# Spread inverses as one transfer per row, and the banks of attention in another order

## The chip, the cores and the metric

The kernel runs on one core of a Trainium2 chip. Its time is the device time of one execution in microseconds (us); the number that counts is the median over executions. Engines are named as in the profile: PE (matmul), PEld (its weight loads), DVE, ACT and POOL (elementwise), SP (here only the issuer of transfers). PSUM, PE's output memory, has eight banks of 128 x 512 float32; every score tile or value tile takes one bank. Transfers between memory and on-chip storage run on 16 DMA engines.

## The reference, cut to what matters

Two attention paths of 16 heads of width 28 over the same 2048 tokens, mixed by a gate. Path A is linear attention, path B softmax attention.

```
def _A_ref(x, wqkv, w_phi, wo):
    ...
    phi_q = concat([softmax(pq), softmax(-pq)]);  phi_k = concat([softmax(pk), softmax(-pk)])
    kv  = einsum("bhsf,bhsd->bhfd", phi_k, v)
    num = einsum("bhqf,bhfd->bhqd", phi_q, kv)
    den = einsum("bhqf,bhf->bhq", phi_q, z)[..., None] + 1e-6
    return merge_heads(num / den) @ wo
def _B_ref(x, wqkv, wo):
    p = softmax(einsum("bhqd,bhkd->bhqk", q, k) * scale)
    return merge_heads(einsum("bhqk,bhkd->bhqd", p, v)) @ wo
g = sigmoid((x * gate_w).sum(-1, keepdims=True))
return g * a + (1 - g) * b
```

## The kernel before

The kernel has three stages. The first (to about 62 us) loads the tokens, splits them into high and low parts and projects queries and keys of path B, which go to memory (`qkd`). The second (62 to 356 us) computes path A token tile by token tile. In its gaps it runs `mx_unit`, which finds the row maxima of path B's scores: PE's `pmd` and `pmb` tiles (L260), ACT's `rl` (L264), DVE's reduction into `part` (L265). Towards its end it computes path B's values (`value_b`, tiles `pvb`, copied out by ACT into `vb`, L699). The third (from 356 us) is attention of path B: scores (`score`, L874), exponentials (L882), remaining row maxima (L288, L295), value products (`values`, L1019), normalisation and the output projection.

The order of work on PE, DVE, ACT and POOL is the order of the code, written out by hand; each engine works through its queue in that order. The order of the transfers on SP is set by a scheduler.

**Path A's normalisation.** Query tiles (128 tokens) are handled in eight pairs. For each pair `numer` computes numerators and denominators into two tiles `pn` (L529), 256 tokens and all heads: a tile has four groups of 32 rows, one head each, of which row 28 is the denominator. `normalize1` copies the tiles to `oU` on ACT (L381) and fetches the denominators by two small transfers into `den` (L384). `normalize2` inverts them on DVE (L389), writes them to a small buffer `rd` in memory, 4 rows of 1024 inverses (L393, two transfers), and spreads them back: `rs` has 128 rows, and each of the 4 rows of `rd` is read 32 times, 512 KB in all (L394). `normalize3` multiplies `oU` by `rs` on DVE (L400). `normalize4` splits the result into high (ACT, L408) and low (POOL, L409) halves, which `out_a` multiplies with the output weights (`poa`, L544). In names of the profile an `a` is added for path A: `dena`, `rda`, `rsa`. Path B uses the same functions for one tile at a time (n = 1, names with `b`); its transfer of 256 KB is a single one before and after. In between, the queues hold other work of path A: query projection (`pq`, L109, copied by ACT to `pcq`, L421), the features `featq` (DVE L423, L424, L443 to L445, POOL L429, L431, L446, ACT's exponential L434), their transposes (`pft`, L516, copied by ACT to `fT`, L519).

**The banks.** Each stage opens its own pool of PSUM tiles. A tag gets its bank when it is first named, and a new pool hands out the banks in turn; the first instruction that writes a bank waits for the last reader of what the old pool had there. In the old pool, the two banks of tag `s` hold the value tiles by turns, and the six of tag `mx` hold those of `mx_unit` and the first four score tiles (`st0`). In the new pool there is `pv` for the value product, and `g0` to `g6`, handed out by the list `free`. The first attention step with scores of its own (s = 1) uses `g0`, `g1`, two row-maximum tiles in `g2` and `g3`, scores in `g4` and `g5`, and a row-maximum tile in `g6`. `pv` is first written by `values(0)`, behind the scores of step 2.

Of the kernel before, what the change touches and what calls it, by code (L numbers as in the profile page):

```python
# [41 lines left out]
def gated_mix_kernel(ctx, tc, xT, wqkB, wvB, wvA, wkAT, wqAT, phi, woA, woB,  # L42
# [7 lines left out]
    nc = tc.nc  # L50
# [336 lines left out]
    def normalize2(pool, oU, den, nm, n):  # L387

        nc.vector.reciprocal(den, den)  # L389
        rd = dr.tile([4, n * 512], F32, tag=f"rd{n}", name=f"rd{nm}", bufs=2)  # L390
        rs = pool.tile([P, n, 512], F32, tag="rs", name=f"rs{nm}", bufs=n)
        for k in range(n):
            nc.sync.dma_start(rd[:, k * 512:(k + 1) * 512], den[:, k, :])  # L393
        nc.sync.dma_start(rs.rearrange("p n q -> p (n q)"),  # L394
                          rd.unsqueeze(1).to_broadcast([4, 32, n * 512]))
        return oU, rs

    def normalize3(oU, rs, n):
# [312 lines left out]
    for i in range(2 * NT + 11):  # L711
        t, q = i, i - NT
# [47 lines left out]
        if y >= 6 and y % 2 == 0 and tb - 3 < 8:  # L760
            num[tb - 3] = normalize2(ta, *num[tb - 3], f"a{tb - 3}", 2)
# [198 lines left out]
    def bank(i, nm):  # L960
        return ps2.tile([P, 512], F32, tag=f"g{i}", name=nm, bufs=1)
# [2 lines left out]
        free.append(free.pop(0))  # L964
        return bank(free[-1], nm)

    for i in (0, None, 1, 6, 5, 4, 3, 2):
        if i is None:
            ps2.tile([P, 512], F32, tag="pv", name="pv_first", bufs=1)
        else:  # L970
            bank(i, f"first{i}")
# [83 lines left out]
    def finish(gq, s):  # L1055
# [8 lines left out]
        def f2():  # L1064
            st["n"] = normalize2(late_p, *st["n"], f"b{gq}", 1)
# [189 lines left out]
```

## Time and profile before

| | us |
|---|---|
| median of 3 executions | 982.85 (982.53 to 985.76) |
| the profiled execution, its time | 983.95 |
| its span, first to last instruction | 982.2 |
| PE busy | 971.7 (99%) |
| ACT busy | 751.9 (77%) |
| DVE busy | 715.5 (73%) |
| POOL busy | 230.6 (23%) |

The durations below come from the profiled execution. A matmul's end is modelled, and matmuls overlap, so a busy PE isn't a PE at its peak; what counts is where it waits, and which wait ends last. The mean granted clock of PE over the span is 0.998 of the full one. In a view of stretches the two figures behind the busy times are the granted clock and the share of the 16 DMA engines that is busy.

### The profile page before, as it was taken

What the parts mean: (1) busy time and instruction counts of PE and PEld (TensorE: products, weight loads), DVE (VectorE), ACT (ScalarE), POOL (GpSimd) and SP (SyncE); (2) the same over time, 40 slices, a digit from 0 to 9 for tenths busy, and PEclk for the clock granted to TensorE, in tenths of its full rate; (3) what the DMA queues carried; (4) which work ended last, traced back from release to release, by engine and by line L of the source; (5) the groups of instructions that cost most, each with busy time, mean ns of one, the idle gap of its engine ahead of it and who ended that gap; (6) DMA issues with size and microseconds to landing.
All of it is one profiled execution on the core that took longest, in us unless ns stands there. A gap on an engine that the chain in (4) does not pass through costs nothing.

```text
span 982.2 us, 22550 instructions
## 1 busy us (share of the span) xinstructions
PE 971.7 (99%) x8510; PEld 602.5 (61%) x8510; DVE 715.5 (73%) x1337; ACT 751.9 (77%) x1442; POOL 230.6 (23%) x237
## 2 busy tenths in 40 slices
PE   9999999998999999999999999999999999999998
PEld 8877877786777655555555555555555555555555
DVE  5476767886755678888888888888888888885112
ACT  5455656586876679889889889889889888887662
POOL 1235535586634800031011011011011011010010
PEclk9999999999999999999999999999999999999999
DMA  8973010112233333121122121122231222100441
GB/s 307 321 244 114 32 54 32 58 36 78 71 115 109 93 119 118 39 58 46 65 86 73 37 61 45 59 79 68 67 83 42 66 61 67 38 21 31 141 150 57
DMA packets 56140, 84.49 MB, mean 86 GB/s; under 512 B 17216, under 2 KB 23984, under 8 KB 56032
## 3 DMA queue, kind: packets, MB, share of 16 engines
q1 hardware_dynamic: 56032, 83.06, 26.9%
q8 instruction: 67, 1.10, 0.4%
q14 instruction: 41, 0.34, 0.1%
HBM read 54.86 MB, written 27.78 MB: 84 GB/s over the span
## 4 chain that ended last, share of the span: by engine, by line
PE 95%; DVE 2%; DMA 1%; ACT 1%; issue 0%; SPq 0%; POOL 0%; DVEq 0%; POOLq 0%; ACTq 0%
PE g L874 29%; PE pv L1019 26%; PE pqk L109 6%; PE poa L544 4%; PE pk L127 4%; PE pva L127 4%; PE g L288 3%; PE pmd L260 3%; PE pob L109 3%; PE pq L109 2%; PE pvb L127 2%; PE pvb L109 2%; PE pqk L635 1%; DMA rsa<-rda 1%; PE pft L516 1%; PE pkv L468 1%
## 5 line engine op out<-in xcount | busy, mean ns | idle before, releaser
L882 ACT ACTIVATE p<-g 128x512 f32<-128x512 f32 x1020 | 525.8, 610 | 83.9 <-PE g L874 83.2
L295 DVE TENSOR_REDUCE part<-g 128x1 f32<-128x512 f32 x704 | 442.6, 684 | 84.9 <-PE g L288 83.0
L874 PEld LDWEIGHTS g<-qst,kst 32*128 32x128 f32 x3060 | 221.3, 182 | 216.4 <-DVE part L295 194.7
L874 PE MATMUL g<-qst,kst 32*128 32x512 f32 x3060 | 338.1, 419 | 1.1 <-ACT vb L699 0.9
L1019 PE MATMUL pv<-p,vb 128*32 128x512 f32 x2048 | 273.0, 604 | 0.0
L288 PE MATMUL g<-kc,qc 28*128 28x512 f32 x704 | 233.3, 494 | 0.0
L265 DVE CUSTOM_DVE_ANT_0 rl<-pmb,rl 128x512 f32<-128x512 f32 x160 | 103.4, 684 | 51.0 <-ACT rl L264 51.0
L400 POOL TENSOR_TENSOR oUb<-oUb,rsb 128x512 f32<-128x512 f32 x15 | 19.3, 1289 | 494.4 <-DMA rsb<-rdb 462.4
L264 ACT ACTIVATE rl<-pmd 128x512 f32<-128x512 f32 x160 | 87.5, 603 | 31.0 <-PE pmb L260 30.1
L288 PEld LDWEIGHTS g<-kc,qc 28*128 28x128 f32 x704 | 86.2, 181 | 0.2
L1019 PEld LDWEIGHTS pv<-p,vb 128*32 128x32 f32 x2048 | 40.5, 108 | 66.2 <-issue 64.9
L109 PE MATMUL pqk<-XH,wB 128*128 128x512 f32 x192 | 59.1, 396 | 0.0
L544 PE MATMUL poa<-woA_s,oTa 128*128 128x448 f32 x192 | 45.7, 386 | 0.0
L573 ACT CAST ev<-pqk 128x512 fp32r<-128x512 f32 x28 | 16.1, 588 | 38.6 <-PE pqk L109 29.6
L1030 DVE SCALAR_TENSOR_TENSOR acc<-pob,gate,acc 128x448 f32<-128x448 f32 x12 | 8.2, 684 | 48.4 <-PE pob L109 48.4
L260 PE MATMUL pmb<-kp,qp 28*128 28x512 f32 x160 | 42.1, 495 | 0.1
L574 DVE TENSOR_TENSOR ev<-pqk,ev 128x512 fp32r<-128x512 f32 x28 | 19.1, 690 | 30.7 <-ACT ev L573 30.7
L109 PEld LDWEIGHTS pqk<-XH,wB 128*128 128x128 f32 x192 | 35.4, 188 | 8.5 <-issue 1.2
L544 PEld LDWEIGHTS poa<-woA_s,oTa 128*128 128x128 f32 x192 | 35.9, 195 | 7.2 <-issue 3.7
L260 PE MATMUL pmd<-kp,qp 28*128 28x512 f32 x160 | 40.0, 494 | 0.0
L127 PE MATMUL pk<-wkA_s,XH 128*128 128x448 f32 x128 | 39.4, 381 | 0.0
L127 PE MATMUL pva<-wvA_s,XH 128*128 128x450 f32 x128 | 37.8, 371 | 0.0
(158 smaller groups left out, 1056.3 us busy)
## 6 DMA issues: line engine op xcount, KB each, us to landing
qkd<-ev SPq DMA_DIRECT2D x28, 512.0 KB
qst<-qkd SPq DMA_DIRECT2D x64, 112.0 KB
kst<-qkd SPq DMA_DIRECT2D x64, 112.0 KB
od<-oTb SPq DMA_DIRECT2D x48, 112.0 KB
rsa<-rda SPq DMA_DIRECT2D x8, 512.0 KB
oL<-od SPq DMA_DIRECT2D x8, 512.0 KB
rsb<-rdb SPq DMA_DIRECT2D x15, 256.0 KB
gad<-ga SPq DMA_DIRECT2D x16, 224.0 KB
```

The costliest lines, as they stand in the source:

```text
L109: nc.tensor.matmul(dst, l, r, start=i == 0, stop=i == len(todo) - 1)
L127: nc.tensor.matmul(dst[:, :n], l, r, start=i == 0, stop=i == len(todo) - 1, skip_group_check=True)
L260: nc.tensor.matmul(pm[j], qc[js, qt * P:(qt + 1) * P], kc[js, :], start=True, stop=True, tile_position=(32 * i, 0))
L264: nc.scalar.activation(rl, pm[i], AF.Relu)
L265: nc.vector.tensor_tensor_reduce(rl, pm[2 + i], rl, 1.0, LOWEST, ALU.add, ALU.max, part[:, col + i:col + i + 1])
L288: nc.tensor.matmul(pm, mxs[("qc", gq)][js, qt * P:(qt + 1) * P], mxs[("kc", gq // NQ, kb)][js, :], start=True, stop=True, tile_position=(3 ...
L295: nc.vector.tensor_reduce(part[:, col:col + 1], pm, AX.X, ALU.max)
L400: (nc.gpsimd if n == 1 else nc.vector).tensor_mul(oU, oU, rs)
L544: nc.tensor.matmul(po[:, :D], l, r, start=i == 0, stop=i == len(todo) - 1, skip_group_check=True)
L874: nc.tensor.matmul(st[j], kst_of[(gq // NQ, kt // 4)][js, k, (kt % 4) * P:(kt % 4 + 1) * P], qst_of[gq][js, q, :], start=n == 0, stop=n == ...
L882: nc.scalar.activation(p, st[j], AF.Exp, scale=SCALE)
L1019: nc.tensor.matmul(pv[32 * j:32 * j + 32, :], vb[kt // 8][:, kt % 8, 4 * g + j, :], pt[j], start=kt == 0, stop=kt == NT - 1, tile_position ...
```

## The change

The spread of a pair's inverses becomes four transfers of 128 KB: for each of the four rows of `rd`, one that reads it 32 times into its 32 rows of `rs`. A tile of its own (n = 1, path B) keeps the single transfer. And the loop that names the banks of attention for the first time runs in another order.

```
         rs = pool.tile([P, n, 512], F32, tag="rs", name=f"rs{nm}", bufs=n)
         for k in range(n):
             nc.sync.dma_start(rd[:, k * 512:(k + 1) * 512], den[:, k, :])
-        nc.sync.dma_start(rs.rearrange("p n q -> p (n q)"),
-                          rd.unsqueeze(1).to_broadcast([4, 32, n * 512]))
+        rows = rs.rearrange("p n q -> p (n q)")
+        if n == 2:
+            for j in range(4):
+                nc.sync.dma_start(rows[32 * j:32 * j + 32],
+                                  rd[j:j + 1].to_broadcast([32, n * 512]))
+        else:
+            nc.sync.dma_start(rows, rd.unsqueeze(1).to_broadcast([4, 32, n * 512]))
         return oU, rs
...
-    for i in (0, None, 1, 6, 5, 4, 3, 2):
+    for i in (None, 0, 6, 5, 4, 3, 2, 1):
         if i is None:
             ps2.tile([P, 512], F32, tag="pv", name="pv_first", bufs=1)
         else:
             bank(i, f"first{i}")
```

Lines behind the edit are five higher in the changed kernel (L874 becomes L879, L400 becomes L405); the spread is L397 there for a pair. SP's queue in path A from the first pair's inverses on, before (`rda` and `dena` are the small transfers, `gad` a store of a result of path A, `qp` a load for the row maxima; the number behind a name is the pair):

```order
L393 DMA rda0_2538<-dena0_2463 4x32x16 x2
L384 DMA dena1_2570<-oUa1_2567 128x1x16 x2
L394 DMA rsa0_2539<-rda0_2538 128x1x1024
L393 DMA rda1_2645<-dena1_2570 4x32x16 x2
L384 DMA dena2_2678<-oUa2_2675 128x1x16 x2
L394 DMA rsa1_2646<-rda1_2645 128x1x1024
L393 DMA rda2_2773<-dena2_2678 4x32x16 x2
L384 DMA dena3_2806<-oUa3_2803 128x1x16 x2
L550 DMA gad0_69<-ga0_2822 128x448
L394 DMA rsa2_2774<-rda2_2773 128x1x1024
L176 DMA qp3_1_2946<-qkd_68 28x512 x4
L550 DMA gad0_69<-ga1_2923 128x448
```

The same place in the changed kernel:

```order
L393 DMA rda0_2538<-dena0_2463 4x32x16 x2
L384 DMA dena1_2573<-oUa1_2570 128x1x16 x2
L397 DMA rsa0_2539<-rda0_2538 32x1024 x4
L393 DMA rda1_2648<-dena1_2573 4x32x16 x2
L384 DMA dena2_2684<-oUa2_2681 128x1x16 x2
L397 DMA rsa1_2649<-rda1_2648 32x1024 x4
L384 DMA dena3_2815<-oUa3_2812 128x1x16
L393 DMA rda2_2779<-dena2_2684 4x32x16 x2
L384 DMA dena3_2815<-oUa3_2812 128x1x16
L555 DMA gad0_69<-ga0_2831 128x448
L397 DMA rsa2_2780<-rda2_2779 32x1024 x4
L176 DMA qp3_1_2955<-qkd_68 28x512 x2
```

The four transfers stand where the one stood; half of the fourth pair's denominators now stands ahead of the third pair's inverses, and `gad` between the two halves of the `qp` loads. Further on, the scheduler moves some `kp` and `kt` loads behind such a store in the same way, up to the end of path A.

PE's first scores of attention, before (in brackets, the engine for whose count an instruction waits; `pvb15` is the last value tile, `g1_0` to `g1_5` are written into `g0` to `g5`):

```order
L127 MATMUL pvb15_4387<-wvB_s_2296,XH_87 128x448 x2
L874 MATMUL g1_0_4449<-qst0_3991,kst0_3993 128x512 [waits Activation_49]
L874 MATMUL g1_1_4450<-qst0_3991,kst0_3993 128x512
L288 MATMUL g1_2_4451<-kc1_0_4117,qc5_4127 128x512 [waits DVE_49]
L288 MATMUL g1_3_4452<-kc1_0_4117,qc5_4127 128x512 [waits DVE_49]
L874 MATMUL g1_0_4449<-qst0_3991,kst0_3993 128x512
L874 MATMUL g1_1_4450<-qst0_3991,kst0_3993 128x512
L874 MATMUL g1_4_4453<-qst0_3991,kst0_3993 128x512
L874 MATMUL g1_5_4454<-qst0_3991,kst0_3993 128x512
```

And in the changed kernel:

```order
L127 MATMUL pvb15_4411<-wvB_s_2296,XH_87 128x448 x2
L879 MATMUL g1_0_4473<-qst0_4015,kst0_4017 128x512 [waits Activation_49]
L879 MATMUL g1_1_4474<-qst0_4015,kst0_4017 128x512 [waits DVE_49]
L288 MATMUL g1_2_4475<-kc1_0_4141,qc5_4151 128x512 [waits DVE_49]
L288 MATMUL g1_3_4476<-kc1_0_4141,qc5_4151 128x512 [waits Activation_49]
L879 MATMUL g1_0_4473<-qst0_4015,kst0_4017 128x512
L879 MATMUL g1_1_4474<-qst0_4015,kst0_4017 128x512
L879 MATMUL g1_4_4477<-qst0_4015,kst0_4017 128x512 [waits Activation_49]
L879 MATMUL g1_5_4478<-qst0_4015,kst0_4017 128x512 [waits Activation_49]
```

No instruction moves here; the waits do. Before, the first score waits for ACT's copy of `pvb15`, the last value tile, and the others of that step need no wait on ACT after that. In the changed kernel the first waits for the copy of `pvb14`, `g1_1` and `g1_2` for DVE's last two reductions of the row maxima, and `g1_3` to `g1_6` in turn for ACT's exponentials of the four `st0` tiles.

## The prediction

> **What bounds the kernel now.** I read the page's busy line and chain first, then the PE's own waits, the chain in order of time, and timelines and stretches around the two places that the change touches.
>
> ```profile
> span 982.2 us, 22550 instructions
> PE 971.7 (99%) x8510; PEld 602.5 (61%) x8510; DVE 715.5 (73%) x1337; ACT 751.9 (77%) x1442; POOL 230.6 (23%) x237
> PE 95%; DVE 2%; DMA 1%; ACT 1%; issue 0%; SPq 0%; POOL 0%; DVEq 0%; POOLq 0%; ACTq 0%
> ...
> PE pn L529 <- ACT fT L519: 3.8, 1, 3.8
> ...
> PE g L874 <- ACT vb L699: 0.9, 1, 0.9
> ```
>
> PE is the bound: 971.7 of 982.2 us, 95% of the chain. The last two rows are two of the four entries in the table of PE's waits; the change can only pay where PE waits. One is in path A (3.8 us), one at the start of attention (0.9). By stretches (start:end, length, busy us of PE, PEld, DVE, ACT and POOL, granted clock, share of the 16 DMA engines, GB/s), PE has no gap from 264 to 328 us, and almost none in attention:
>
> ```profile
> 264.00:328.00 64.00, 64.00 (x404) 49.10 (x402) 35.51 (x94) 42.60 (x85) 29.05 (x26) 1.00 0.32 102
> 358.00:600.00 242.00, 241.89 (x2420) 126.51 (x2417) 204.79 (x338) 217.01 (x420) 23.23 (x24) 1.00 0.21 64
> 600.00:900.00 300.00, 299.94 (x2994) 155.75 (x2988) 253.65 (x420) 268.69 (x520) 26.76 (x25) 1.00 0.20 57
> ```
>
> So a microsecond won ahead of these stretches should reach the end: whatever follows is released by PE, not by a date.
>
> **Part 1, the spread inverses.** The chain (start, us, what) passes through the first pair's spread:
>
> ```profile
> 215.06 1.91 DMA rda<-dena
> 217.02 9.39 DMA rsa<-rda
> 226.50 1.24 DVE oUa L400
> 230.27 1.15 PE pn L529 x32
> 231.42 4.20 PE poa L544 x12
> ...
> 247.38 2.65 PE poa L544 x12
> ```
>
> The 512 KB transfer takes 9.39 us to land. The engines around it (start, us, engine, line, and in brackets the idle time before and its releaser):
>
> ```profile
> 221.54 0.33 DVE L445 TENSOR_TENSOR fsumq<-fsumq,featq 128x16 f32<-128x16 f32 x1
> 226.50 1.22 DVE L400 TENSOR_TENSOR oUa<-oUa,rsa 128x1024 f32<-128x1024 f32 x1 [4.62 <-DMA rsa<-rda]
> 227.64 0.61 DVE L423 TENSOR_REDUCE extq<-pcq 128x16 f32<-128x448 f32 x1
> 222.95 0.54 ACT L421 COPY pcq<-pq 128x448 f32<-128x448 f32 x1 [1.13 <-PE pq L109]
> 227.76 1.14 ACT L408 CAST oTa<-oUa 128x512 fp32r<-128x512 f32 x2 [4.27 <-DVE oUa L400]
> 229.65 1.05 ACT L519 COPY fT<-pft 128x512 f32<-128x512 f32 x2
> 225.96 0.49 PE L260 MATMUL pmb<-kp,qp 28*128 28x512 f32 x2
> 230.27 1.15 PE L529 MATMUL pn<-fT,KV 57*32 57x256 f32 x32 [3.82 <-ACT fT L519]
> 230.13 2.52 POOL L409 TENSOR_TENSOR oTa<-oUa,oTa 128x512 fp32r<-128x512 f32 x2
> ```
>
> DVE stands at L400 for 4.62 us, ACT behind it at L408, and PE at L529 for 3.82 us, because the fT copy is queued on ACT behind L408. How fast will four transfers land? The rows for that, stretches first, then SP's issues:
>
> ```profile
> 222.00:223.00 1.00, 1.00 (x8) 0.89 (x7) 0.00 (x0) 0.05 (x1) 0.94 (x1) 1.00 0.26 82
> 321.00:321.50 0.50, 0.50 (x4) 0.24 (x2) 0.00 (x0) 0.00 (x0) 0.00 (x0) 1.00 0.41 119
> 323.50:324.00 0.50, 0.50 (x4) 0.46 (x3) 0.50 (x3) 0.00 (x0) 0.50 (x1) 1.00 0.68 255
> ...
> 217.02 0.54 SPq L394 DMA_DIRECT2D rsa<-rda  x1
> 220.31 1.14 SPq L393 DMA_DIRECT2D rda<-dena  x2
> 320.08 0.74 SPq L176 DMA_DIRECT2D kt<-qkd  x2
> ```
>
> While the old transfer runs, the DMA share is 0.26: a quarter of 16 engines, four, as many as the rows it copies, at 82 GB/s. The two kt loads (28 rows of 2 KB each, at 321 us) get 0.41 and 119 GB/s, a 128-row store (323.5) 0.68 and 255. A transfer of 32 rows of 4 KB has no reason in these rows to stay on one engine or on four. Issuing costs SP 0.37 (kt, 0.74/2) to 0.54 us (rsa) each, so the fourth goes out at 217.02 + 3 x 0.37..0.54 = 218.1..218.6. Add 1.91 for a small transfer to land (rda) and 128 KB at 255 GB/s, 0.51 us: 220.6 to 221.1. The slow end, all four in turn at 119 GB/s (1.10 us each), is 217.02 + 1.91 + 4.4 = 223.3. I take the first, since two kt loads end before they can fill the engines and four transfers overlap: landed before 221.87, when DVE comes free (221.54 + 0.33). L400 then waits for nothing.
>
> What is late next? ACT's copy L421 ends at 223.49, and L408 cannot start earlier (from L400 alone it would be 221.9 + 1.26 = 223.2), so ACT moves up 227.76 - 223.49 = 4.27 us. fT starts at 225.38 and pn could start at 226.00, but PE is busy until 225.96 + 0.49 = 226.45. PE itself is last, and the 3.82 us of idle are gone, with 0.45 us in reserve. The output product poa then starts 1.15 later, at 227.60, and needs L409's halves on POOL. L409 moves with DVE's L423, which is bounded by the same copy (223.49 + 0.06): 4.09 us earlier, so it starts at 226.04 and its halves end at 227.3 and 228.56. poa's matmuls take 2.65/12 = 0.22 us; the third (228.04) and the sixth (228.70) are the first to need them. Nothing new waits, the second with 0.14 us to spare.
>
> There is a second term. After its idle time PE ran at half clock:
>
> ```profile
> 232.00:233.00 1.00, 1.00 (x4) 0.87 (x4) 1.00 (x2) 1.00 (x3) 1.00 (x2) 0.50 0.25 102
> ```
>
> The 12 matmuls of poa took 4.20 there and 2.65 in the same group at 247.38: 1.55 us for the granted clock of 0.50 alone. In other rows quoted here the clock is 1.00, so I take the dip as the price of the idle time and count it as gone with it. Between ends: 0 (it comes anyway) and 1.55; I take 1.55, since it begins right behind the gap.
>
> The other seven pairs: none of them holds PE (its table of waits has no other row in path A), so their faster landing earns nothing. Take one of them, and the pool's margin further on:
>
> ```profile
> 252.33 0.53 SPq L394 DMA_DIRECT2D rsa<-rda  x1
> 264.99 1.22 DVE L400 TENSOR_TENSOR oUa<-oUa,rsa 128x1024 f32<-128x1024 f32 x1
> 327.02 0.95 POOL L833 MEMSET qst<- 128x1024 f32 x1 [1.39 <-PE poa L544]
> ...
> L400 DVEq EVENT_SEMAPHORE  x3: 21/21/21, 226.4 to 311.5; - x3
> ```
>
> 12.66 us lie between issue and use, against 9.39 for landing. The costs: SP issues three more transfers a pair, 3 x 0.37..0.54 = 1.1 to 1.6 us. Behind the first pair's stands rda of the second, which waits for DVE until 220.31 anyway; SP is through at 219.2 at the latest. Further on the order on SP moves some loads of path B's queries and keys (qp, kp and kt) behind stores of path A's results (gad). They feed POOL's subtractions and score tiles much later, POOL idles 1.39 us at L833 after the last of these subtractions, and PE has no gap in 264 to 328: I cost it at nothing, 1.6 us if that cover were gone. L400 waits on up to three more semaphores, 0.02 us each: below 0.1, and inside the DVE's idle time. Part 1: 3.82 + 1.55 = **5.4 us**.
>
> **Part 2, the bank order.** The last value tiles and the first scores:
>
> ```profile
> 354.11 0.54 ACT L699 COPY vb<-pvb 128x448 f32<-128x448 f32 x1
> 354.99 0.08 DVE L265 DVE_READ_ACCUMULATOR2_ANT part<- 128x1 f32 x1
> 355.26 2.07 ACT L882 ACTIVATE p<-st 128x512 f32<-128x512 f32 x4 [0.61 <-PE st L874]
> 356.30 0.56 PE L127 MATMUL pvb<-wvB_s,XH 128*128 128x448 f32 x2
> 357.18 0.57 ACT L699 COPY vb<-pvb 128x448 f32<-128x448 f32 x1
> 357.80 0.50 PE L874 MATMUL g<-qst,kst 32*128 32x512 f32 x2 [0.94 <-ACT vb L699]
> ```
>
> PE ends the last value tile at 356.86 and waits 0.94 us for its copy out, because g0 takes that tile's bank. In the changed order g0 takes the bank of the tile before it (copied out by 354.65), g1 and g2 wait for DVE's last accumulations (355.07), g3 to g6 for ACT's first four exponentials, which end one by one until 357.33. PE reaches g3 at about 356.9 (the first exponential ends near 355.8) and g6 as the last of 15 matmuls. So all are free. The last tile's bank goes to pv, first written two steps later. PE gains **0.94 us**; what follows, DVE's and ACT's first reads of attention, hangs on PE's scores and moves along. Bounds: 0, if something else holds g0, and 1.10, if the matmuls' spacing of 0.2 us counts rather than their modelled end.
>
> **The sum.** 5.37 + 0.94 = 6.3 us. The profiled execution took 983.95 us with a span of 982.2, 1.1 above the median of 982.85; its span should become 975.9, and the median 982.85 - 6.3 = **976.5 us**.
>
> **The rivals.**
> A: the split doesn't spread. Then the last row lands when it did, 226.41, or up to 1.6 us later by the extra issues, and only the 0.94 us of part 2 is left: 981.9 us (983.5 with the late issues). For it: no row shows 32 copies read from one 4 KB row. Against: the share of 0.26 with four rows, and 0.41 with 28. The Trainium skill has a rule against this change: "DMA: Bandwidth & Descriptors", Rules for kernel authors, says not to bother splitting a transfer by partitions, since the parts serialize on the same 16 engines; by it, too, the time would be 981.9. The same page (Why a DMA increments its semaphore by 16 and not by 1) says that a transfer uses the largest number of engines up to 16 that divides the slowest dimension of both sides, 4 before and 16 after; by that rule the forecast holds, and the trace agrees with its first half (0.26). Chance 8%.
> B: it spreads, but reads slower, at 119 GB/s or less. Landing at 223.3 leaves L400 a wait of 1.4, PE an idle time of about 0.7, and 977.2 us; towards 82 GB/s it runs into A. Chance 8%, mostly below 979.6.
> C, slower: 16 engines that read one 4 KB row are served one after another. One engine read its row at 82/4 = 20.5 GB/s; if a row gives no more to all of them, 128 KB takes 6.4 us, four rows 25.6, and the first pair lands at 244.5 instead of 226.41: 18.1 us later, 1000 us even if the other pairs hid theirs. It decides from a rate below 62 GB/s, where the loss passes the gain of part 2. Against: the 82 to 102 GB/s above (the second pair's spread runs at 232 us) come from 16 KB that lie together. Chance 6%.
> D: the idle time goes, but SP's later loads reach path B's score tiles too late. Three sets of kp and kt loads stand behind the spreads of the last pairs; at 1.6 us each PE loses up to 4.8 us of the gain: 981.3, at half of it 978.9. Against it: PE has no gap there and POOL has 1.39 us to spare. Chance 4%.
>
> **How the numbers follow.** The forecast has 74%. About 0.3%, 2.9 us, is what a measurement of this kernel can tell from no change, so faster means below 979.9. Faster: the forecast, 6 of B's 8% and 3 of D's 4%, 0.83; same: A, the rest of B and of D, 0.11; slower: C, 0.06. The range goes down to 976.5 - 0.2 (part 2 at 1.10) - 1.1 (the distance between the profiled run and the median) = 975.2, and up to the middle between B's 977.2 and A's 981.9, 979.6, which takes in part 2 at zero and the clock term at zero (978.0).
>
> **What would show it.** In the profile after: DMA share well above 0.26 for a short time after 217; DVE's L400 with no wait for rsa, near 222; no PE wait at pn L529; the first poa group at 2.65, clock 1.00 throughout; at the start of attention no wait of g for the vb copy. The forecast is wrong if rsa still takes over 5 us (part 1 fails at the spread), or if a new wait, such as PE waiting for POOL at poa or for kp at pmd, appears between 230 and 356 (it fails at what is late next).

## The result, and the profile after

The changed kernel takes 977.81 us (median of 6 executions, 976.81 to 978.27), the kernel before 983.16 beside it (6 executions, 982.53 to 985.76). The ratio is 0.9939, 95% interval 0.9926 to 0.9952: between 4.7 and 7.3 us faster. The two medians lie 5.4 us apart, the two means 6.0. The forecast was 976.5 (975.2 to 979.6). The profiled execution took 976.95 us, 7.0 less than the profiled one of before.

The head of the page, and all that is left in the table of PE's waits (us in total, times, longest):

```profile
span 975.1 us, 22588 instructions
PE 969.6 (99%) x8510; PEld 600.4 (62%) x8510; DVE 715.9 (73%) x1337; ACT 751.6 (77%) x1442; POOL 232.1 (24%) x237
...
PE pqk L623 <- POOL ident masks.py:199: 1.4, 1, 1.4
```

The waits at `pn` (3.8 us) and at the first `g` (0.9) are gone, and no other has taken their place; 1.4 us at the kernel's first matmuls were there before. The stretches in which the four transfers of the first pair run, and the two long ones behind them (granted clock, DMA share and GB/s at the end of a row):

```profile
218.00:219.00 1.00, 1.00 (x34) 0.47 (x33) 0.96 (x3) 0.82 (x2) 0.81 (x2) 1.00 0.89 303
219.00:220.00 1.00, 1.00 (x16) 0.84 (x8) 1.00 (x3) 1.00 (x2) 1.00 (x2) 1.00 0.78 193
220.00:221.00 1.00, 0.89 (x5) 0.77 (x5) 1.00 (x2) 1.00 (x4) 1.00 (x2) 1.00 0.01 0
259.00:323.00 64.00, 64.00 (x403) 49.10 (x402) 34.90 (x94) 42.57 (x85) 29.63 (x26) 1.00 0.33 102
353.00:595.00 242.00, 242.00 (x2414) 126.26 (x2414) 204.68 (x339) 217.13 (x421) 23.20 (x24) 1.00 0.22 65
```

The 512 KB that took 9.39 us to land, at a share of about 0.26, are through in about 2 us at 0.89 and 0.78; at 220 the DMA engines are empty. What this does to the engines (timeline, then the same place in the chain):

```profile
216.81 1.80 SPq L397 DMA_DIRECT2D rsa<-rda  x4
221.59 1.21 DVE L405 TENSOR_TENSOR oUa<-oUa,rsa 128x1024 f32<-128x1024 f32 x1
222.73 0.54 ACT L426 COPY pcq<-pq 128x448 f32<-128x448 f32 x1 [1.13 <-PE pq L109]
223.16 1.15 ACT L413 CAST oTa<-oUa 128x512 fp32r<-128x512 f32 x2
225.06 1.06 ACT L524 COPY fT<-pft 128x512 f32<-128x512 f32 x2
225.74 0.49 PE L260 MATMUL pmb<-kp,qp 28*128 28x512 f32 x2
226.16 1.09 PE L534 MATMUL pn<-fT,KV 57*32 57x256 f32 x32
...
226.23 1.02 PE pn L534 x32
227.26 2.83 PE poa L549 x12
...
241.85 2.65 PE poa L549 x12
```

DVE's multiplication (L405) stands without a wait, as does ACT's cast (L413), and `pn` follows `pmb` on PE at once: PE is bound by its own work, as the prediction said of what is late next. The first group of `poa` took 2.83 us at full clock instead of 4.20.

The start of attention:

```profile
350.87 0.57 PE L127 MATMUL pvb<-wvB_s,XH 128*128 128x448 f32 x2
351.37 0.50 PE L879 MATMUL g<-qst,kst 32*128 32x512 f32 x2
351.72 0.57 ACT L704 COPY vb<-pvb 128x448 f32<-128x448 f32 x1
```

The first scores now begin at 351.37, ahead of the last copy of `vb` (351.72), for which they waited before.

### The profile page after: what moved, and what is told of

Its sections match the earlier page's. It is cut to its first block, busy times and chain, and to the rows that moved or that the text cites. A ratio compares the mean times of both kernels' runs of the same rounds, so it can differ in the third digit from the quotient of the medians.

```text
span 975.1 us, 22588 instructions
## 1 busy us (share of the span) xinstructions
PE 969.6 (99%) x8510; PEld 600.4 (62%) x8510; DVE 715.9 (73%) x1337; ACT 751.6 (77%) x1442; POOL 232.1 (24%) x237
## 4 chain that ended last, share of the span: by engine, by line
PE 95%; DVE 2%; DMA 1%; ACT 1%; issue 0%; POOL 0%; SPq 0%; DVEq 0%; POOLq 0%
PE g L879 29%; PE pv L1024 27%; PE pqk L109 5%; PE pk L127 4%; PE poa L549 4%; PE pva L127 4%; PE g L288 4%; PE pmd L260 3%; PE pob L109 3%; PE pq L109 3%; PE pvb L127 2%; PE pvb L109 2%; PE pqk L640 1%; PE pft L521 1%; PE pkv L473 1%; DMA qkd<-ev 1%
## 5 line engine op out<-in xcount | busy, mean ns | idle before, releaser
L879 PEld LDWEIGHTS g<-qst,kst 32*128 32x128 f32 x3060 | 221.2, 182 | 215.5 <-DVE part L295 194.5
L879 PE MATMUL g<-qst,kst 32*128 32x512 f32 x3060 | 338.0, 419 | 0.1
L405 POOL TENSOR_TENSOR oUb<-oUb,rsb 128x512 f32<-128x512 f32 x15 | 19.3, 1287 | 492.8 <-DMA rsb<-rdb 459.5
```

What stands on the lines that cost most here:

```text
L405: (nc.gpsimd if n == 1 else nc.vector).tensor_mul(oU, oU, rs)
L879: nc.tensor.matmul(st[j], kst_of[(gq // NQ, kt // 4)][js, k, (kt % 4) * P:(kt % 4 + 1) * P], qst_of[gq][js, q, :], start=n == 0, stop=n == ...
```

## The experiments

"Before" is the kernel before on the same chip; its executions lie between 981.1 and 987.1 us there, with medians of 984.31, 984.46 and 984.29 in the three groups (e1 to e4; e5 to e7; e8 and e9). Why they scatter is part of what these runs show.

**e1: the split alone.** The bank loop is back in its old order:

```
-    for i in (None, 0, 6, 5, 4, 3, 2, 1):
+    for i in (0, None, 1, 6, 5, 4, 3, 2):
```

> The split alone, banks named as before. My theory (the two parts add, each worth what its own wait cost): PE's wait at pn and the half clock behind it are gone, the wait of g for the last vb copy stays at 0.9 us; time 5.4 us below before (ratio about 0.9945). Rival (the parts overlap: what the first wins, the second wait takes back): all of the gain of the changed kernel is here already, ratio 0.994 and no wait at g; or the gain is smaller than 4 us because the later start of attention absorbs it.

Measured: 977.83 us (977.70 to 980.21), ratio 0.9945 (0.9929 to 0.9960). The wait of `g` is back, that of `pn` isn't. The time can't decide between the theory (0.9945) and the rival (0.994), but the rival had no wait at `g`, and that wait stands. In its profile the half clock appears at another place than before, behind this wait:

```profile
PE g L879 <- ACT vb L704: 0.9, 1, 0.9
...
354.00:356.00 2.00, 1.89 (x13) 1.19 (x12) 2.00 (x4) 1.98 (x4) 0.00 (x0) 0.88 0.34 110
356.00:358.00 2.00, 2.00 (x13) 0.78 (x13) 1.39 (x3) 1.61 (x5) 0.00 (x0) 0.50 0.38 135
358.00:360.00 2.00, 2.00 (x23) 0.70 (x15) 0.41 (x2) 0.55 (x2) 0.00 (x0) 0.77 0.18 63
```

What is lacking to full clock, 0.12 + 0.50 + 0.23 of 2 us each, is 1.7 us of PE's work, or half clock for 3.4 us. Two of six executions had a mean clock of 0.997 and took 980.1 and 980.2; four had 1.0 and took 977.7 to 977.9. So 0.9 us of idle time can bring on half clock, in some executions and not in others, and those take about 2.4 us longer, of which the clock accounts for 1.7.

**e2: the bank order alone,** in the kernel before.

> The bank order alone, one transfer per pair as before. My theory: PE waits 3.8 us at pn as before, clock 0.5 behind it, no wait of g for the vb copy; time 0.9 us below before (ratio 0.999). Rival (another wait takes the place of that one): no change at all, with a wait of g for DVE or for the exponentials of st0.

Measured: 981.56 us (979.90 to 984.58, 12 executions), ratio 0.9980 (0.9968 to 0.9992). The wait of `g` is gone and that of `pn` stands: each part removes its own wait. Its profile also shows what the one of before could not, that the single transfer doesn't always take 9.39 us (waits, chain, stretches):

```profile
PE pn L529 <- ACT fT L519: 2.1, 1, 2.1
...
216.73 7.69 DMA rsa<-rda
...
229.45 4.19 PE poa L544 x12
...
228.00:230.00 2.00, 1.71 (x35) 0.97 (x36) 1.93 (x5) 2.00 (x5) 2.00 (x3) 0.97 0.30 106
230.00:232.00 2.00, 2.00 (x7) 1.73 (x6) 2.00 (x8) 1.95 (x4) 2.00 (x3) 0.50 0.25 102
232.00:234.00 2.00, 2.00 (x10) 1.76 (x10) 1.93 (x5) 0.32 (x1) 1.77 (x3) 0.68 0.11 19
```

It landed in 7.69, PE idled 2.1 us instead of 3.8, and the half clock followed all the same, again for 2 x (0.03 + 0.50 + 0.32) / 0.5 = 3.4 us.

**e3: four transfers for the first pair only,** one for the other seven.

```
-        if n == 2:
+        if nm == "a0":
```

> The split for the first pair alone, the other seven with one transfer, new bank order. My theory (only the first pair holds PE): the same time as the changed kernel within 0.5 us. It may cost a little at the second pair, whose transfer takes 7 to 9 us again but is now wanted some 5 us earlier in time: it is issued near 222.7, lands near 231 and is wanted near 231.1. Rival (all eight pairs earn): half of the gain or more is lost, 3 us slower than the changed kernel.

Measured: 977.39 us (976.75 to 978.05), ratio 0.9936 (0.9922 to 0.9950): all of the gain. PE has no wait but the one at its first matmuls. That the other pairs' transfers land faster earns nothing.

**e4: as many transfers, on four engines.** Each of the four transfers names its row 4 x 8 times instead of 32 times, so that its slowest dimension is 4:

```
-                                  rd[j:j + 1].to_broadcast([32, n * 512]))
+                                  rd[j:j + 1].unsqueeze(1).to_broadcast([4, 8, n * 512]))
```

> The same four transfers of 32 rows, but their source is written as 4 x 8 copies, so that a transfer's slowest dimension is 4 and not 32; new bank order. My theory (the gain is the number of engines that share the work): DMA share 0.25 again, the last row lands 9 to 10.5 us after the first issue, DVE waits 4.5 to 6 us at the product, PE 3.8 to 5 us at pn, half clock behind; time as with the bank order alone, or up to 1.5 us longer (982 to 984). Rival (the gain is the finer transfers, which overlap in flight): as the changed kernel, 977.8.

Measured: 980.92 us (980.04 to 982.97), ratio 0.9972 (0.9962 to 0.9982). Waits, a stretch and the chain:

```profile
PE pn L534 <- ACT fT L524: 2.8, 1, 2.8
...
222.00:223.00 1.00, 1.00 (x6) 0.89 (x5) 0.16 (x1) 0.10 (x1) 0.81 (x2) 1.00 0.28 86
...
219.31 6.23 DMA rsa<-rda
225.73 1.24 DVE oUa L405
```

Four transfers, the share back at 0.28 and 86 GB/s, the wait back at `pn`. It isn't the number of transfers that counts but the shape of each: four transfers with a slowest dimension of 4 together get the share of four engines, no more. The sizes were forecast too large: the last row landed at 225.54, 8.2 us after the first issue at 217.30 (forecast 9 to 10.5), `pn` waited 2.8 us (forecast 3.8 to 5), and the time lies below the 982 to 984 expected. Four of the eleven executions had a mean clock of 1.0, the others less.

**e5: the same with 8 x 4.**

```
-                                  rd[j:j + 1].to_broadcast([32, n * 512]))
+                                  rd[j:j + 1].unsqueeze(1).to_broadcast([8, 4, n * 512]))
```

> The same four transfers, source written as 8 x 4 copies (slowest dimension 8). My theory (engines in proportion): DMA share about 0.5, the data of a pair moves in 2.5 to 3.5 us, the last row lands about 5.5 us after the first issue, near 222.3; DVE waits 0.3 to 1 us at the first product, PE not at all or under 0.5 us; time as the changed kernel within 0.7 us. Rival (16 engines or nothing): the time of the bank order alone, 982.

Measured: 978.00 us (977.16 to 978.44), ratio 0.9934 (0.9919 to 0.9949).

```profile
PE pn L534 <- ACT fT L524: 0.6, 1, 0.6
...
219.00:220.00 1.00, 1.00 (x22) 0.71 (x7) 1.00 (x3) 0.98 (x2) 0.82 (x1) 1.00 0.52 188
220.00:221.00 1.00, 0.88 (x6) 0.63 (x5) 1.00 (x3) 1.00 (x3) 1.00 (x3) 1.00 0.43 172
...
219.28 3.88 DMA rsa<-rda
```

Half the share, and some 0.6 of the rate; the last row lands at 223.2, later than expected for this run (222.3) and at the slow end that the prediction had set (223.3). PE idles 0.6 us, just over the 0.5 expected, where rival B had said 0.7. The mean clock was 1.0 in all four executions.

**e6: two transfers of two rows each,** with a slowest dimension of 2, for every pair:

```
-            for j in range(4):
-                nc.sync.dma_start(rows[32 * j:32 * j + 32],
-                                  rd[j:j + 1].to_broadcast([32, n * 512]))
+            for j in (0, 2):
+                nc.sync.dma_start(rows[32 * j:32 * j + 64],
+                                  rd[j:j + 2].unsqueeze(1).to_broadcast([2, 32, n * 512]))
```

> Two transfers a pair, each with two rows of 32 copies (slowest dimension 2). My theory (two engines carry all of it): share 0.12, 512 KB at about 41 GB/s, 12.8 us, so the first pair lands near 231.6 and later pairs too late as well; PE idles 8 us or more at the first pair, and the kernel is 12 to 35 us slower than before. Rival (finer transfers help by their number): between before and the changed kernel, 978 to 982.

Measured: 1006.07 us (1004.66 to 1008.12), ratio 1.0222 (1.0204 to 1.0240).

```profile
PE pn L534 <- ACT fT L524: 7.3, 1, 7.3
PE pmb L260 <- DVE part L265: 6.0, 2, 5.3
...
221.00:222.00 1.00, 1.00 (x5) 0.94 (x6) 0.97 (x2) 1.00 (x3) 1.00 (x2) 1.00 0.14 57
...
231.82 12.55 DMA rsa<-rda
...
290.00:298.00 8.00, 6.67 (x17) 5.36 (x18) 3.38 (x10) 3.79 (x8) 3.30 (x4) 0.57 0.34 116
338.00:346.00 8.00, 7.48 (x21) 5.19 (x22) 2.71 (x8) 3.83 (x8) 5.79 (x5) 0.57 0.29 96
```

More transfers than before, and 22 us slower: a share of 0.14, two engines of 16, at 57 GB/s. The second pair's spread (at 231.82) takes 12.55 us; DVE stands in front of it, and PE's row maxima (`pmb`) stand behind DVE. Waiting is only about half of the loss. PE's waits sum to some 10 us more than before; and in this profile the half clock comes four times, for 10.2, 3.4, 6.8 and 6.8 us (the last two are the stretches from 290 and 338), which takes about 9 us more of PE's work than before.

**e7: a size between.** For the first pair, rows 0 to 2 with a slowest dimension of 4, row 3 with 16; all other pairs with 16.

```
+                e = 16 if nm != "a0" or j == 3 else 4
...
-                                  rd[j:j + 1].to_broadcast([32, n * 512]))
+                                  rd[j:j + 1].unsqueeze(1).to_broadcast([e, 32 // e, n * 512]))
```

> As the changed kernel, but for the first pair rows 0 to 2 go through four engines and row 3 through 16. My theory: 384 KB through four engines land about 7.8 us after the issue, near 224.6; DVE waits 2.9 us at the first product, PE about 2 us at pn. If the half clock needs an idle time near the 3.8 us of before, the clock stays at 1.00 and the time is 2 us above the changed kernel (979.9). Rival (any idle time there brings the half clock): the first poa group takes about 4.2 us instead of 2.65, and the time is 3.6 us above (981.4).

Measured: 979.91 us (978.50 to 981.72), ratio 0.9957 (0.9941 to 0.9974).

```profile
PE pn L535 <- ACT fT L525: 1.7, 1, 1.7
...
219.12 5.22 DMA rsa<-rda
```

The median hits the forecast, but as a mix of two levels: three executions at clock 1.0 took 978.5 to 979.4, three at 0.997 to 0.998 took 980.5 to 981.7. The same kernel, with about the same idle time, pays the half clock in one execution and not in the next.

**e8 and e9: PE's idle time filled, nothing else changed.** What was open was whether the half clock is the price of the idle time. Into the kernel before go 16 (e8) or 8 (e9) matmuls of no use, ahead of the `pn` that is held:

```
         pn = [(ps_mx if tb < 2 else ps_s)(f"pn{tb}_{i}") for i in range(2)]
+        if tb == 3:
+            for _ in range(16):
+                nc.tensor.matmul(pn[0][:, :D], XH[:, 0, :P], wqA_s[:, 0, 0, :D],
+                                 start=True, stop=True)
```

> The kernel before, with 16 idle matmuls (128 x 448, as pq's; about 0.20 us each, 3.2 in all) written into the first pn tile ahead of the first pair's held pn; their result is overwritten. They lie inside PE's wait of 3.8, so they should not move pn. Theory (the half clock is the price of PE's idle time): no stretch at half clock behind pn, poa near 2.8 instead of 4.20, the clock of all runs at 0.999 to 1.0, and the time at the level of the best executions of the kernel before, 981.5 (980.8 to 982.3), with a spread under 1.5 us. Rival (the half clock comes by itself, whatever PE did before): the clock stays at 0.995 to 0.999, the median within 1 us of the kernel before, 984, and its spread of 4 us and more remains.

Measured: 982.68 us (981.51 to 985.48, 12 executions), ratio 0.9991 (0.9980 to 1.0002). Timeline, waits and stretches:

```profile
227.29 3.51 PE L527 MATMUL pn<-wqA_s,XH 128*128 128x448 f32 x16
229.13 1.05 ACT L519 COPY fT<-pft 128x512 f32<-128x512 f32 x2
230.74 1.09 PE L533 MATMUL pn<-fT,KV 57*32 57x256 f32 x32
231.76 2.73 PE L548 MATMUL poa<-woA_s,oTa 128*128 128x448 f32 x12
...
PE g L878 <- ACT vb L703: 0.9, 1, 0.9
...
232.00:234.00 2.00, 2.00 (x11) 1.83 (x11) 2.00 (x7) 1.40 (x3) 2.00 (x4) 1.00 0.17 68
...
358.00:360.00 2.00, 1.94 (x13) 1.62 (x15) 1.77 (x4) 1.81 (x4) 0.00 (x0) 0.69 0.35 110
360.00:362.00 2.00, 2.00 (x17) 0.49 (x11) 1.42 (x3) 1.79 (x4) 0.00 (x0) 0.50 0.39 130
362.00:364.00 2.00, 2.00 (x20) 1.00 (x15) 0.29 (x1) 0.27 (x1) 0.00 (x0) 0.50 0.18 61
364.00:366.00 2.00, 2.00 (x19) 0.37 (x11) 1.69 (x3) 1.51 (x4) 0.00 (x0) 0.61 0.26 69
```

With PE busy through the gap the clock stays at 1.00 behind it, and `poa` takes 2.73: the theory held at this place. But in this execution the half clock sits behind the 0.9 us of `g` instead, which this kernel still has, and for twice as long: 2 x (0.31 + 0.50 + 0.50 + 0.39) / 0.5 = 6.8 us. So the expectation of a narrow spread failed: seven of twelve executions had clock 1.0, the others 0.996 to 0.999, and even the seven took from 981.5 to 983.6. The median lies above the 980.8 to 982.3 expected. The 16 matmuls, 3.5 us long, did not lie inside the wait as expected either: before, `pn` began 0.62 us after ACT began to copy `fT` (230.27 against 229.65); here that would be 229.75, and the added matmuls hold it until 230.74, about 1.0 us. That takes back part of what the clock gives. The interval of the ratio takes in 1: by its time this kernel doesn't show a gain.

> The same with 8 idle matmuls (1.6 us), which leaves PE about 2.2 us of idle time behind them. If the half clock goes with the length of one idle stretch, about as in the kernel with four transfers on four engines (idle 2.8: eight of eleven runs below clock 1.0) and the one with three rows on four engines (idle 1.7: three of six): some runs at 1.0 and 981.5, others at 0.996 to 0.998 and 983 to 984.5, median 982 to 983.5. By the rival: as the kernel before, 984.

Measured: 982.02 us (981.14 to 984.08, 12 executions), ratio 0.9986 (0.9976 to 0.9997). In the profiled execution the transfer landed in 7.67 us, so that 0.3 us of idle time were left, and the clock stayed at 1.00; four of twelve executions were at 0.998. (For e4 the expectation counts eight of eleven executions below clock 1.0; it was seven.) The 0.9 us of `g` stood here too, without half clock behind it. The median lies at the low end of the range expected, but the landing time, which moves by 1.7 us from one execution to the next, keeps this run from telling how the price goes with the length.

## Why the prediction was right

Its sign, its range and its mechanism held; the time came out 1.3 us above the forecast. Its steps, by the two profiled executions (the changed one is 0.2 us ahead when it issues the first spread, 216.81 against 217.02; this is taken off the first pair's figures):

- **The split spreads.** The forecast was 220.6 to 221.1 for the last row; the DMA engines are empty by 220. That refutes rival A (and B, by the rate of 303 GB/s against 119), and e4 beside the changed kernel shows why: four transfers in both, 0.28 and 0.89 of the engines, ratios to before of 0.9972 (0.9962 to 0.9982) and 0.9939 (0.9926 to 0.9952). The rule of the Trainium skill against splitting by partitions ("DMA: Bandwidth & Descriptors", Rules for kernel authors), whose reason is that both parts spread over all 16 engines, doesn't hold for this transfer, which at a share of 0.26 used only part of them. The same page of the Trainium skill (Why a DMA increments its semaphore by 16 and not by 1) gives the number of engines as the largest number up to 16 that divides the slowest dimension of both sides. The traces agree where a slowest dimension was set here: 2, 4, 8 and 32 gave shares of 0.14, 0.26 to 0.28, 0.43 to 0.52 and 0.78 to 0.89.
- **Rival C, a row that can't be read by many engines at once,** is refuted: four 4 KB rows, each read 32 times, moved at 303 GB/s.
- **Part 1.** Forecast 3.82 + 1.55 = 5.37. `pn` comes 4.11 - 0.21 = 3.9 earlier, and `poa` takes 4.20 - 2.83 = 1.4 less: 5.3. The 1.4 is short of 1.55 by what the prediction took for a margin: it gave `poa`'s sixth matmul 0.14 us to spare against POOL, and the weight load waits there:

```profile
PEld poa L549 <- POOL oTa L414: 0.3, 1, 0.3
```

- **Part 2.** Forecast 0.94. The last value matmuls start 356.30 - 350.87 = 5.43 earlier, the first scores 357.80 - 351.37 = 6.43: 1.0.
- **Nothing is given back** (rival D): PE is full in 64.00 of 64.00 us from 259 on, and its table of waits has no row behind the kernel's first matmuls, with SP's three more issues a pair (1.80 us for the four).
- **What the sum lacked.** The last matmuls come 0.3 us earlier than these terms say in the course of 600 us of attention, and another 0.3 at its end, where PE's wait at `pd`, 0.2 us before, is gone; the first 0.3 is not traced to any row. This row of before was not in the prediction:

```profile
969.70 0.66 PE L1106 MATMUL pd<-ident,oUlast 128*128 128x128 f32 x4 [0.19 <-DVE oUlast L1102]
```

The step that was mis-sized is the clock term, and with it the step from the profiled execution to the median. The prediction took one stretch of half clock, worth 1.55 us, as the fixed price of 3.82 us of idle time, and subtracted the profiled execution's gain from the median. The runs show both sizes to vary. The single transfer lands in 7.7 to 9.4 us (before, e2, e9), so that `pn` waits 2.1 to 3.8. The half clock lasts 3.4 us or twice that (once, in e6, three times), a price of 1.7 or 3.4 us where PE has work all through it. And the half clock comes in some executions and not in others, behind either of the two waits. In the 57 executions of before beside the experiments, those with a mean clock of 0.999 or more (7) took 981.1 to 982.4 us, those with 0.995 to 0.998 (50) 982.2 to 987.1. All 15 executions of the three kernels with both waits gone or at most 0.6 us long (the changed one, e3, e5) had 0.999 or 1.0 and lie between 976.75 and 978.44; the 0.999 of the changed kernel's profile comes from its last 1.4 us, behind PE's last matmul. The profiled execution of before had waited its full 3.8 us and lost 7.0 us to the one after; the medians of the runs beside each other are 5.4 us apart. So some luck lay in which execution was profiled: an estimate from e2's rows, 2.1 us of wait and 4.19 - 2.65 = 1.5 for the clock, would have given part 1 as 3.6 and a forecast of 978.3.

So the cause is shown for both parts, part 2 more surely in the trace than in the time: e1 and e2 each take away one wait, e3 places part 1 in the first pair, e4 to e7 move the landing by the shape of the transfer alone, and the wait of PE follows: 0 in the changed kernel, then 0.6 (e5), 1.7 (e7), 2.8 (e4) and 7.3 us (e6). That idle time brings on the half clock is shown for the first gap (filled in e8, clock 1.00 and `poa` at 2.73; unfilled in before, e2 and e4, clock 0.50), not when it does. The counts over all executions agree: nine of twelve in e8 and eight of twelve in e9 had a mean clock of 0.999 or more, against 7 of 57 in before. For the 0.9 us of `g` it rests on where the half clock stands in two profiles (e1, e8); in two others (before, e9) the same wait has none behind it. The Trainium skill ("TensorE: Matmul & The Clock Gate", What's actually happening) has a free-running window of activity of about 3.4 us, which would make the same gap count in one execution and not in another; that agrees with e7's two levels, and the half clock's length of 3.4 us (e1, e2) and 6.8 (e8) is one and two such windows. In e6 the four stretches of half clock, read at 0.01 us, begin at 229.32, 249.80, 290.76 and 338.54, which lie 6, 12 and 14 steps of 3.413 us apart, as such a window would have it. The rule of thumb on the same page of the Trainium skill (HAM oscillation), no idle gaps over about 3.4 us, doesn't protect here: the half clock stands behind 2.1 us in e2 and behind 0.9 in e1 and e8.

How much part 2 is worth in the median stays less sure than in the trace: e2 alone gained 0.8 to 3.1 us by its interval; e1, without part 2, has a ratio (0.9945) that can't be told from the changed kernel's (0.9939), and only two of its six executions were some 2.4 us longer than the others.

## What to carry to other kernels

Read a slow transfer's DMA share against 16 engines before its size: a share of 0.26 is about four engines, and where that is also the size of the transfer's outermost dimension, it points to its shape. Reshaping (one transfer per row, or more copies outermost) is worth it only for the transfer that some engine waits for; here one of eight. Where PE runs without a gap, a short idle time may cost another 1.7 us through its clock (3.4 us at half), so even a small wait for a PSUM bank can be worth naming the banks by hand. And a profile is one execution: forecast the median from several, since a wait on a transfer and the clock behind it both move by a microsecond or two.

## What the hardware showed that was not expected

- Half clock after short idle times: 0.50 of the clock, for 3.4 us (before, e1, e2, e4) or 6.8 (e8), behind an idle time of 0.9 (e1, e8), 2.1 (e2), 2.8 (e4) and 3.8 us (before), each beginning 1.2 to 2.5 us after PE had resumed; none behind 0.6 (e5), nor behind 1.7 in e7's profiled execution, nor behind the 0.9 of `g` in those of before and e9. In e6, behind a wait of 7.3 us, it began before PE resumed. What decides is open beyond the steps of 3.413 us on which e6's stretches lie: by the same steps from before's half clock (231.48), 0.9 us of its wait at `g` falls within one step, and none follows.
- A 4 KB row in memory can be read by many engines at once without a loss that these runs show: 303 GB/s at a share of 0.89, more than the 255 GB/s at 0.68 of the 128-row store.
- PE's wait of 0.2 us at `pd`, at the end of the kernel, stands in the four profiles of kernels with a single transfer per pair (before, e2, e8, e9) and in none of the seven with several for at least the first pair. DVE's copy ahead of it begins 0.4 us after the last value product in before, and 0.1 in the changed kernel. Why is open.
